# A fixed order for the first 888 operations, product sums in common banks, and the last sums behind the join of two paths

## The chip, the cores and the metric

The kernel runs on one core of one Trainium2 chip. The metric is the device time of one execution in microseconds (us), from the launch to the end of the program. Its engines work side by side, each through its own queue in the order of the program: TensorE (PE) multiplies, VectorE (DVE), ScalarE (ACT) and GpSimd (POOL) work on elements, and SyncE (SP) issues transfers. They wait for each other by semaphores.

## The reference

Attention over 2 batches, 8 heads, 768 positions and 64 numbers per head; a query sees the first 8 keys (global) and the 96 keys that end at its own position (local). Two feed-forward networks follow, on 1536 tokens.

```python
scores = scale * np.matmul(q, k.transpose(0, 1, 3, 2))
keep = is_global | is_local          # pos < 8, or 0 <= rel < 96
dist = np.where(is_global & ~is_local, float(n_local), np.abs(rel))
scores = np.where(keep, scores - slopes[:, None, None] * dist, -1e9)
a = np.exp(scores - np.max(scores, axis=-1, keepdims=True))
a = a / (np.sum(a, axis=-1, keepdims=True) + 1e-09)
x = np.matmul(a, v)                  # then (B, S, H*D): 1536 tokens x 512
h = x @ w_in                         # 512 -> 2048
x = np.where(h > 0, h, np.exp(np.minimum(h, 0)) - 1) @ w_out     # 2048 -> 512
h = x @ w2_in
out = (h * (1 / (1 + np.exp(-1.702 * h)))) @ w2_out
```

`n_global` and `n_local` are inputs too; the kernel reads them on the chip.

## The kernel before

**Products.** Every number of a feed-forward product is split in a high and a low part of a fast 32-bit format, and each product is three matmuls (high by high, high by low, low by high). The weights come as 64-bit floats and are converted on the chip, 128x512 at a time (`conv`): a copy of the upper words into `m` (L414 on ACT or L415 on DVE), three bit operations on DVE (L417, L419, L421), the high part (L247 or L248) and the low part (L254).

**Attention.** There are 12 rows of 128 queries, each in two halves of four heads: 24 units (`Band.unit`). A unit is a chain through the engines: scores (PE, small tiles of 64x64, L345), minus the distance with its minimum (DVE, L670), exponential with its sum (ACT, L674), the sum plus 1e-9 in the small tile `st` (DVE or POOL, L677), its reciprocal (DVE, L680), four scalings of `E` (DVE or POOL, L259), transposes (PE, L693 to L699), copies into `pt` (ACT or DVE, L706), the products with the values (PE, L727 on 128x64 tiles, then L738 on 64x64 tiles), and the split into `xh`, `xl`.

**Feed-forward.** Each network has 4 groups of 512 hidden numbers, each group 3 chunks of 512 tokens. `A` (L447) makes 4 hidden tiles, `B` (L487) sums them onto `acc` or `d` by an add on DVE (L508). The first group's work of chunks 0 and 1 is planned among the attention, so that PE has full tiles (128x128) to multiply while a unit's chain runs elsewhere.

**What sets the order.** `Plan` collects operations as nodes with a due time, one or several engines with a modelled cost, and what they read and write. `run` emits them one by one: the earliest modelled start, among near ones the earliest due; `place` also gives a PSUM bank. The modelled times are in `START`, `WAIT`, `TIMES` and the costs. Where PE would be idle in the model, `idle` emits matmuls on zeros ("fillers", L772) that no one reads. Every engine then works its instructions in this order, however long they really take. Of the 8 banks, 5 are dealt out; bank 5 is kept for the last part of the transposes (`tb`, two halves in turn), banks 6 and 7 for the sums of the products with the values (`xb`).

**The beginning and the end.** `start` sets up distances and slopes and tests `n_global` and `n_local` into `n_flag`; the engines load it (L981) and branch (L986) to `banded`, the path of the profile, or to `general`. At the end of a path each engine jumps to where the paths join; behind it stand only the drains and the last barrier of the program (L1033). The last chunk's four sums are added and stored at the end of the path, the fourth in two halves.

Of the kernel before, what the change touches and what calls it, by code (L numbers as in the profile page):

```python
# [11 lines left out]
F32 = mybir.dt.float32  # L12
# [23 lines left out]
ROW0 = 4.9, 5.8  # L36
# [5 lines left out]
SPARE = 0  # L42
# [18 lines left out]
class Bank:  # L61


    def __init__(self):
        self.left = 0
        self.free_at = 0.0
        self.tile = None


class Node:  # L70
# [3 lines left out]
ENGINES = ("PE", "ACT", "DVE", "POOL", "SP")  # L74
BIAS = dict(DVE=1.373, ACT=0.264, POOL=0.0)
WAIT = {
    "PE": dict(PE=0.0, ACT=0.2, DVE=0.2, POOL=0.22, SP=0.2),
    "ACT": dict(PE=0.27, ACT=0.1, DVE=0.15, POOL=0.17, SP=0.2),
    "DVE": dict(PE=0.25, ACT=0.13, DVE=0.13, POOL=0.16, SP=0.2),
    "POOL": dict(PE=0.2, ACT=0.08, DVE=0.07, POOL=0.02, SP=0.2),  # L80
    "SP": dict.fromkeys(ENGINES, 0.1),
}


class Plan:
# [7 lines left out]
    def __init__(self, k):  # L93
        self.k = k
        self.writer, self.readers = {}, {}
        self.done_at = {}
        self.fill = None
        self.dma = 8.8
        self.avail = dict(START)
        self.banks = [(0.0, i) for i in range(8)]  # L100
        self.pending = {}
        self.cand = {e: [] for e in self.avail}
        self.mode = "full"

    def node(self, due, opts, reads=(), writes=(), alloc=None, uses=(), spare=None, mode="full"):
        n = Node()
        n.mode = mode
# [47 lines left out]
    def at(self, n, e):  # L155
        t = max(n.ready[e], self.avail[e])
        if n.alloc:
# [4 lines left out]
    def run(self):  # L162
        while self.pending:
# [35 lines left out]
    def idle(self, t):  # L199
# [4 lines left out]
        while at + step < t and free[0] + 0.2 <= at:  # L204
# [3 lines left out]
    def place(self, t, e, n):  # L208
# [3 lines left out]
        for b in n.alloc:  # L212
            free = min(self.banks)
# [29 lines left out]
def o_copy(k, out, in_, n, psum=False):  # L243
# [3 lines left out]
        ("ACT", n / 1200 + (0.05 if psum else 0.09), lambda: nc.scalar.activation(out, in_, AF.Copy)),  # L247
# [9 lines left out]
def o_scale(k, out, in_, c, n):  # L257

    op = lambda e: lambda: e.tensor_scalar(out, in_, c, 1.0, ALU.mult, ALU.mult)  # L259
    return [("DVE", n / 1940 + 0.13, op(k.nc.vector)), ("POOL", n / 760 + 0.268, op(k.nc.gpsimd))]  # L260


def start(k, ns, load):
# [9 lines left out]
    lim, off, k.slope = small(2, "n_lim"), small(1, "n_off"), small(H, "slope")  # L273
# [19 lines left out]
    for e in k.E:  # L293
        G.memset(e[:, :, QW:256], 0.0)
# [10 lines left out]
    k.f, k.n, a, c = small(4, "n_f"), small(2, "n_val"), small(2, "n_a"), small(2, "n_c")  # L305
    flag, k.ns = small(1, "n_flag", I32), small(1, "n_scaled")
    V.tensor_copy(k.f, raw)
    V.scalar_tensor_tensor(k.n, k.f[:, 1:4:2], float(2.0 ** 32), k.f[:, 0:4:2], ALU.mult, ALU.add)
    k.ng, k.nl = k.n[:, 0:1], k.n[:, 1:2]
    V.scalar_tensor_tensor(a, k.n, 1.0, lim, ALU.mult, ALU.is_le)  # L310
    for x in range(2):
        V.scalar_tensor_tensor(c[:, x:x + 1], k.n[:, x:x + 1], float(x), a[:, x:x + 1], ALU.is_ge,
                               ALU.mult)
    V.tensor_tensor(flag, c[:, 0:1], c[:, 1:2], ALU.mult)
    V.tensor_scalar(k.ns, k.nl, 1.0 / BIG, 1.0, ALU.mult, ALU.mult)
    V.tensor_scalar(k.big, col, k.ng, 1.0, ALU.is_ge, ALU.mult)
    V.scalar_tensor_tensor(w, own, k.ns, k.big, ALU.is_ge, ALU.mult)
    V.scalar_tensor_tensor(k.d0, own, k.ns, w, ALU.min, ALU.add)
    return flag
# [35 lines left out]
class FFN:  # L355
# [35 lines left out]
    def conv(self, due, G, kind, f):  # L391
# [7 lines left out]
        else:  # L399
# [23 lines left out]
        node(due + 2.5, o_copy(k, hi, mf, 512), [km], khi)  # L423
        node(due + 3, o_sub(k, lo, mf, f32(hi), 512), [km] + khi, klo)

    def A(self, due, G, c, f, t0=0, n=TC):
# [23 lines left out]
        for kk in range(KK):  # L450
            node(due + n / 850 * kk, [("PE", n / 751, lambda kk=kk: mm(kk), 3 * n)],
# [18 lines left out]
    def B(self, due, G, c, m, t0=0, n=TC, late=GF - 1):  # L470
# [5 lines left out]
        b = Bank()  # L476
# [13 lines left out]
        for f in range(GF):  # L490
# [3 lines left out]
            node(at, [("PE", n / 751, lambda f=f: mm(f))],  # L494
# [6 lines left out]
        sc = 1.0 if G < NG else 0.5  # L501
        if g == 0:
# [5 lines left out]
        node(due, [("DVE", n / 960 + 0.07, lambda: V.scalar_tensor_tensor(  # L508
            acc, o(), sc, acc, ALU.mult, ALU.add))], [b] + ka, ka, uses=[b])
# [7 lines left out]
        else:  # L517
            r0 = c * TC + m * 128
            node(due + 0.5, [("SP", 0.33, lambda: nc.sync.dma_start(
                out=self.out[r0:r0 + 128, t0:t0 + n], in_=acc), 0.9)], ka)  # L520
# [28 lines left out]
class Band:  # L549

    def __init__(self, k, plan, pool):
# [5 lines left out]
        self.plan.banks = [(0.0, b) for b in range(5)]  # L557
        self.tb, *self.xb = [Bank() for _ in range(3)]
        for x, b in enumerate((self.tb, *self.xb)):
            b.bank, b.tile = 5 + x, k.bank[5 + x]  # L560
# [11 lines left out]
    def dist(self):  # L572
# [4 lines left out]
        def window():  # L577
            V = nc.vector
            V.scalar_tensor_tensor(base, k.rel, k.ns, k.rel, ALU.is_ge, ALU.add)
            for x in (96, QW + 32):  # L580
                V.tensor_scalar(base[:, x:x + NGLOB], k.big[:, 0:NGLOB], k.ns, 1.0,
                                ALU.max, ALU.mult)

        node(11, [("DVE", 0.65, window)], [("e", 0), ("gt", 1)], [("gt", 0)])
        for n in range(H):
            x = n % 2 * QW
            self.slope(12 + n, k.d[:, n, 0:QW], base[:, x:x + QW], n, QW, [("gt", 0)], [("d", n)])
# [9 lines left out]
    def load(self, r, due):  # L597
        k, node = self.k, self.plan.node
        p = r % 2
        if r < 2:  # L600
            self.plan.given((4.4, 7.0)[r], *self.keys(r))
        else:
            node(due, [("SP", 0.4, lambda: k.load_row(r), 1.6)], writes=self.keys(r))
        if r == 0:
            self.plan.given(8.8, ("v", 0))
            self.plan.given(4.9, "d0")
# [430 lines left out]
```

## Time and profile before

| what | value |
|---|---|
| three runs, median (lowest to highest) | 605.40 us (605.22 to 605.52) |
| profiled execution | 605.43 us |
| its span, first to last instruction | 603.5 us |
| PE busy | 593.2 us (98%), 3675 matmuls |
| DVE busy | 388.9 us (64%) |
| ACT busy | 302.8 us (50%) |
| POOL busy | 68.7 us (11%) |
| DMA | 49.46 MB, mean 82 GB/s |

The profiled execution has 1.9 us outside its span. Busy shares are means over two very different parts: the attention runs until about 109 us, with all four engines at work, and from there only the feed-forward networks are left.

### The profile page before, as it was taken

Reading aid. Unit: us, or ns where it says so; the run is one execution under the profiler, and the core shown is the slowest. Engines: PE = TensorE matmul, PEld = TensorE weight load, DVE = VectorE, ACT = ScalarE, POOL = GpSimd, SP = SyncE. Lnnn points to the kernel's source line nnn. Section 1 sums busy time; section 2 is a strip of 40 time slices with the busy share of each in tenths; the row PEclk is TensorE's granted clock in tenths of the full one; section 3 lists DMA queues with packets and bytes.
Section 4 is the critical chain, followed back from the end, with each engine's and each line's share of the span. In section 5 each row is a group of like instructions: output and inputs, shape, how many; then the busy total and the mean of one; then the engine's idle time right before and its main releaser. Section 6 shows DMA issues by size and latency. Waiting matters only on the chain.

```text
span 603.5 us, 9600 instructions
## 1 busy us (share of the span) xinstructions
PE 593.2 (98%) x3675; PEld 491.0 (81%) x3675; DVE 388.9 (64%) x840; ACT 302.8 (50%) x679; POOL 68.7 (11%) x162
## 2 busy tenths in 40 slices
PE   8999999999999999999999999999999999999996
PEld 6788888888888888888888888888888888888885
DVE  8999896177546983499558953577348843843432
ACT  6998898367245454256447643553324521531220
POOL 7787463000000000000000000000000000000000
PEclk9999999999999999999999999999999999999999
DMA  7666562024201340033002230143003320101012
GB/s 248 227 210 205 159 214 75 1 71 140 71 0 36 109 135 0 1 107 135 38 1 71 98 112 0 36 137 107 1 1 104 106 70 1 35 1 70 18 53 76
DMA packets 20582, 49.46 MB, mean 82 GB/s; under 512 B 1968, under 2 KB 7856, under 8 KB 20528
## 3 DMA queue, kind: packets, MB, share of 16 engines
q1 hardware_dynamic: 20368, 48.51, 24.2%
q8 instruction: 31, 0.51, 0.4%
q10 hardware_dynamic: 160, 0.26, 0.2%
q14 instruction: 23, 0.19, 0.1%
HBM read 45.62 MB, written 3.15 MB: 81 GB/s over the span
## 4 chain that ended last, share of the span: by engine, by line
PE 94%; POOL 3%; DVE 2%; issue 1%; ACT 0%; DVEq 0%; POOLq 0%
PE bank L487 43%; PE bank L447 43%; PE bank L345 2%; PE bank L727 2%; POOL E L259 2%; PE bank L696 1%; PE bank L738 1%; PE bank L699 1%; PE bank L772 0%; DVE E L670 0%; POOL row L621 0%; ACT pt L706 0%; PE bank L693 0%; DVE d L259 0%; POOL st L677 0%
## 5 line engine op out<-in xcount | busy, mean ns | idle before, releaser
L447 PE MATMUL bank<-xh,wbig 128*128 128x512 f32 (+1 forms) x560 | 173.6, 381 | 0.9 <-ACT pt L706 0.5
L447 PEld LDWEIGHTS bank<-xh,wbig 128*128 128x128 f32 x560 | 104.0, 188 | 22.0 <-issue 1.6
L447 PE MATMUL bank<-xl,wbig 128*128 128x512 f32 (+1 forms) x280 | 105.5, 377 | 0.0
L487 PE MATMUL bank<-g,wbig 128*128 128x512 f32 (+1 forms) x360 | 80.8, 367 | 0.2
L447 PE MATMUL bank<-xh,kT 128*128 128x512 f32 x240 | 76.3, 389 | 0.0
L487 PEld LDWEIGHTS bank<-g,wbig 128*128 128x128 f32 x360 | 62.8, 188 | 11.9 <-ACT pt L706 0.3
L508 DVE SCALAR_TENSOR_TENSOR acc<-bank,acc 128x512 f32<-128x512 f32 x48 | 33.2, 692 | 54.0 <-PE bank L487 53.9
L463 ACT ACTIVATE e<-bank 128x512 f32<-128x512 f32 x48 | 28.5, 594 | 68.2 <-PE bank L447 68.1
L447 PEld LDWEIGHTS bank<-xl,wbig 128*128 128x128 f32 x280 | 52.7, 188 | 9.4
L487 PE MATMUL bank<-wbig,g 128*128 128x512 f32 (+1 forms) x246 | 59.8, 384 | 0.0
L254 DVE TENSOR_TENSOR g<-gt,g 128x512 fp32r<-128x512 f32 (+1 forms) x70 | 46.6, 666 | 18.8 <-ACT g L247 17.6
L247 ACT ACTIVATE g<-gt 128x512 fp32r<-128x512 f32 (+1 forms) x70 | 42.6, 609 | 25.0 <-DVE gt L465 15.2
L247 ACT ACTIVATE wbig<-m 128x512 fp32r<-128x512 f32 x39 | 24.6, 630 | 58.2 <-PE bank L447 37.6
L465 DVE SCALAR_TENSOR_TENSOR gt<-e,bank 128x512 f32<-128x512 f32 x48 | 32.9, 685 | 31.1 <-ACT e L463 30.7
L487 PEld LDWEIGHTS bank<-wbig,g 128*128 128x128 f32 x246 | 45.4, 188 | 9.1
L447 PEld LDWEIGHTS bank<-xh,kT 128*128 128x128 f32 x240 | 45.1, 188 | 9.3
L259 POOL TENSOR_SCALAR E<-E,st 128x192 f32<-128x192 f32 (+2 forms) x79 | 47.0, 609 | 9.4 <-DVE st L680 4.7
L460 DVE SCALAR_TENSOR_TENSOR gt<-e,bank 128x512 f32<-128x512 f32 (+1 forms) x52 | 33.4, 643 | 22.1 <-ACT e L458 21.7
L447 PE MATMUL bank<-xl,kT 128*128 128x512 f32 x120 | 46.7, 389 | 0.0
L254 DVE TENSOR_TENSOR wbig<-m,wbig 128x512 fp32r<-128x512 f32 x44 | 30.1, 688 | 23.7 <-ACT wbig L247 22.9
L419 DVE SCALAR_TENSOR_TENSOR raw<-raw 128x512 int32<-128x512 int32 x64 | 44.6, 697 | 0.7
L421 DVE SCALAR_TENSOR_TENSOR m<-m,raw 128x512 int32<-128x512 int32 x64 | 44.3, 692 | 0.9
(129 smaller groups left out, 896.4 us busy)
## 6 DMA issues: line engine op xcount, KB each, us to landing
raw<-in_w1i_dram SPq DMA_DIRECT2D x16, 512.0 KB, 3.5
raw<-in_w1o_dram SPq DMA_DIRECT2D x16, 512.0 KB, 3.4
raw<-in_w2i_dram SPq DMA_DIRECT2D x16, 512.0 KB, 3.3
raw<-in_w2o_dram SPq DMA_DIRECT2D x16, 512.0 KB, 3.3
row<-in_qk_dram SPq DMA_DIRECT2D x9, 512.0 KB, 4.8
v<-in_v_dram SPq DMA_DIRECT2D x12, 256.0 KB, 3.9
va<-in_v_dram SPq DMA_DIRECT2D x10, 256.0 KB, 4.1
out_dram<-acc SPq DMA_DIRECT2D x8, 256.0 KB, 2.0
```

Source lines behind the costliest of these rows:

```text
L247: ("ACT", n / 1200 + (0.05 if psum else 0.09), lambda: nc.scalar.activation(out, in_, AF.Copy)),
L254: return [("DVE", n / 960 + 0.068, lambda: nc.vector.tensor_tensor(out, a, b, ALU.subtract))]
L259: op = lambda e: lambda: e.tensor_scalar(out, in_, c, 1.0, ALU.mult, ALU.mult)
L345: k.nc.tensor.matmul(banks[y // 2 * 2 + x][to, y % 2 * n:y % 2 * n + n], lhsT=v[rows, pr, q + 64 * x:q + 64 * x + 64], rhs=v[rows, pr, c:c ...
L419: node(due + 1, [("DVE", 0.6, lambda: V.scalar_tensor_tensor(top, bot, 29, top, ALU.logical_shift_right, ALU.bitwise_or))], [kr], [kr])
L421: node(due + 1.5, [("DVE", 0.6, lambda: V.scalar_tensor_tensor(m, m, 3, top, ALU.logical_shift_left, ALU.bitwise_or))], [km, kr], [km])
L447: nc.tensor.matmul(h(), lhsT=w[:, kk, :], rhs=x[:, kk, :], start=(kk == 0 and j == 0), stop=(kk == KK - 1 and j == 2))
L460: node(due + 1, [("DVE", n / 960 + 0.07, lambda: V.scalar_tensor_tensor(gt, e, -1.0, h(), ALU.add, ALU.max))], [ke, b], [kg], uses=[b])
L463: node(due, [("ACT", n / 1200 + 0.05, lambda: S.activation(e, h(), AF.Tanh, scale=0.851))], [b], [ke], uses=[b])
L465: node(due + 1, [("DVE", n / 960 + 0.07, lambda: V.scalar_tensor_tensor(gt, e, 1.0, h(), ALU.add, ALU.mult))], [ke, b], [kg], uses=[b])
L487: nc.tensor.matmul(o(), lhsT=lhsT, rhs=rhs, start=(f == 0 and j == 0), stop=(f == GF - 1 and j == 2))
L508: node(due, [("DVE", n / 960 + 0.07, lambda: V.scalar_tensor_tensor(acc, o(), sc, acc, ALU.mult, ALU.add))], [b] + ka, ka, uses=[b])
```

## The change

It has four parts.

1. `ORDER` lists the first 888 operations by number, with a letter for the engine where there is a choice (p, a, v, g, s for PE, ACT, DVE, POOL, SP); `run` places these as listed and plans the rest as before. `START`, `WAIT`, `ROW0`, `TIMES` and several costs have new values, by which the due times of the rest, the fillers and the banks come out. More operations may choose: ACT for the scalings of `E`, POOL for two steps of `conv` in the first group.
2. No bank is kept for `tb` and `xb`. Transposes take two banks and the sums of a row take two from the common eight, and the two keys that kept transposes and products in the order of the units are gone.
3. `start` makes the slopes by one shift of integers on DVE from a POOL iota, in place of 16 POOL memsets, tests the limits on raw integers, and writes two new tables of limits on POOL.
4. The adds and stores of the last chunk's third and fourth sum (`held`) are emitted behind the join of the two paths, for which they have fixed banks.

```diff
-TIMES = (7.0, 3.3, 2.8)
+TIMES = (6.0, 3.3, 3.0)
-START = dict(PE=5.3, ACT=5.0, DVE=5.2, POOL=6.0, SP=5.0)
+START = dict(PE=6.6, ACT=5.05, DVE=5.45, POOL=5.05, SP=5.0)
+ORDER = """
+598 41g 9a 107 0 32a 18g 605 38a 61a 156 12a 35g 10 59 4a 110v 60v 11 13 2g 62 15v 14 19 5g 16
...
+"""
     def run(self):
+        for word in self.order:
+            n = self.nodes[int(word.rstrip(LETTERS))]
+            e = ENGINES[LETTERS.index(word[-1])] if word[-1] in LETTERS else n.opts[0][0]
+            n.spare = 0
+            self.place(self.at(n, e), e, n)
         while self.pending:
...
-    for x, most in enumerate((NGLOB, NWIN + 1)):
-        G.memset(lim[:, x:x + 1], float(most))
-    for n in range(H):
+    for to, values in ((most, (NGLOB, NWIN + 1)), (least, (0, 1))):
+        G.memset(to, 0.0)
         for x in range(2):
-            h = n // 2 * 2 + (n % 2 ^ x)
-            G.memset(k.slope[64 * x:64 * x + 64, n:n + 1], -BIG * 2.0 ** (2 - h))
+            G.memset(to[:, 2 * x:2 * x + 1], float(values[x]))
+    for x in range(2):
+        iota(shift[64 * x:64 * x + 64].rearrange("p (a b) -> p a b", b=2),
+             pattern=[[-2, NP], [2 * x - 1, 2]], base=256 + 127 + 38 + 2 - x, channel_multiplier=0)
...
+    V.tensor_scalar(bits, shift, 23, None, ALU.logical_shift_left)
     V.tensor_scalar(rel, rel, off, 1.0 / BIG, ALU.subtract, ALU.mult)
...
+        slow = [] if G else [
+            ("POOL", 0.66, lambda: nc.gpsimd.tensor_scalar(mf, topf, sc, 1.0, ALU.mult, ALU.mult)),
+            ("POOL", 0.66, lambda: nc.gpsimd.tensor_copy(hi, mf))]
...
+        held = (G, c) == (2 * NG - 1, NCH - 1) and m > 1
+        b = Bank(m + 3 + (t0 > 0) if held else None)
...
+        if held:
+            b.left += 1
+            k.held.append((add, store))
+            return
...
-        self.plan.banks = [(0.0, b) for b in range(5)]
-        self.tb, *self.xb = [Bank() for _ in range(3)]
...
-            node(due + 2.3, o_scale(k, e, e, st[:, 12 + n:13 + n], Ws[x]),
-                 [(kE, n), (kst, 12)], [(kE, n)])
-        ta, tb, ktb = Bank(), self.tb, ("tb", u % 2)
+            c = st[:, 12 + n:13 + n]
+            node(due + 2.3, o_scale(k, e, e, c, Ws[x]) + [("ACT", Ws[x] / 1200 + 0.19, lambda e=e, c=c:
+                 nc.scalar.activation(e, e, AF.Copy, scale=c))], [(kE, n), (kst, 12)], [(kE, n)])
+        ta, tb = Bank(), Bank()
...
-             [ta, ktb, "turn"], alloc=ta, uses=[ta, tb], spare=0)
+             [ta, tb], alloc=[ta, tb], uses=[ta, tb], spare=0)
...
+        plan.order = ORDER.split()
         plan.run()
...
+    for add, store in k.held:
+        add()
+        store()
```

**POOL at the start of the program.** `e` holds the distances by iota, `n_lim` the two limits and `slope` the slopes of the heads; `ident` is the identity for the transposes. Before:

```order
L278 IOTA e_97 128x128
L286 MEMSET n_lim 128x1 x2
L290 MEMSET slope 64x1 x16
masks.py:197 MEMSET ident 128x128
masks.py:199 AFFINE_SELECT ident<-ident 128x128
```

After (`n_shift` is the iota from which DVE shifts the slopes):

```order
L339 IOTA e_97 128x128
L347 MEMSET n_most 128x4
L349 MEMSET n_most 128x1 x2
L347 MEMSET n_least 128x4
L349 MEMSET n_least 128x1 x2
L339 IOTA n_shift 64x8 x2
masks.py:197 MEMSET ident 128x128
```

On DVE the shift that reads `n_shift` (L358) now stands ahead of the first operation on `e`, which before stood first (L295) and needs only the iotas of `e`.

**PE in the later attention, one unit's products between the matmuls of a hidden tile.** `pt` holds the transposed weights of a unit, `v` and `va` the values; L447 and L513 are feed-forward matmuls, L696 and L768 transposes. Before:

```order
L447 MATMUL bank_69<-xh_77,wbig 128x512
L727 MATMUL bank_72<-pt_216,va_106 64x64 x2
L727 MATMUL bank_73<-pt_216,v_104 64x64 x2
L727 MATMUL bank_72<-pt_216,va_106 64x64 x2
L727 MATMUL bank_73<-pt_216,v_104 64x64 x2
L738 MATMUL bank_72<-pt_216,v_104 64x64 x2
L738 MATMUL bank_73<-pt_216,va_106 64x64 x2
L738 MATMUL bank_72<-pt_216,v_104 64x64 x2
L738 MATMUL bank_73<-pt_216,va_106 64x64 x2
L696 MATMUL bank_67<-ident,E_102 128x128 x4
L699 MATMUL bank_71<-ident,E_102 128x128 x2
L447 MATMUL bank_68<-xh_77,wbig 128x512
```

After, the end of a run of four units' products (two rows of queries, with banks of their own):

```order
L811 MATMUL bank_70<-pt_205,v_104 64x64 x2
L811 MATMUL bank_73<-pt_205,va_106 64x64 x2
L799 MATMUL bank_70<-pt_206,va_106 64x64 x2
L799 MATMUL bank_73<-pt_206,v_104 64x64 x2
L799 MATMUL bank_70<-pt_206,va_106 64x64 x2
L799 MATMUL bank_73<-pt_206,v_104 64x64 x2
L811 MATMUL bank_70<-pt_206,v_104 64x64 x2
L811 MATMUL bank_73<-pt_206,va_106 64x64 x2
L811 MATMUL bank_70<-pt_206,v_104 64x64 x2
L811 MATMUL bank_73<-pt_206,va_106 64x64 x2
L513 MATMUL bank_68<-xh_76,kT 128x512
```

Before, each unit's products in this stretch stand between full tiles; after, those of several units stand in one run. Counted in the order of the whole path, PE changes between full and small tiles 85 times before and 69 times after.

**DVE at the end of the program.** The last adds, and the jump to the join (L986, L1063). Before:

```order
L508 SCALAR_TENSOR_TENSOR d<-bank_71,d 128x512
L508 SCALAR_TENSOR_TENSOR d<-bank_72,d 128x512
L508 SCALAR_TENSOR_TENSOR d<-bank_73,d 128x512
L508 SCALAR_TENSOR_TENSOR d<-bank_66,d 128x256
L508 SCALAR_TENSOR_TENSOR d<-bank_68,d 128x256
L986 UNCONDITIONAL_BRANCH
```

After:

```order
L575 SCALAR_TENSOR_TENSOR d<-bank_68,d 128x512
L575 SCALAR_TENSOR_TENSOR d<-bank_71,d 128x512
L1063 UNCONDITIONAL_BRANCH
L575 SCALAR_TENSOR_TENSOR d<-bank_71,d 128x512
L575 SCALAR_TENSOR_TENSOR d<-bank_72,d 128x256
L575 SCALAR_TENSOR_TENSOR d<-bank_73,d 128x256
L1113 UNCONDITIONAL_BRANCH
```

Three adds stand behind the jump, and so do three stores on SP; a second jump follows on both.

## Rows read from the trace of the kernel before

**Rows 1.** Page, part 4: share of the chain of work by engine.

```profile
PE 94%; POOL 3%; DVE 2%; issue 1%; ACT 0%; DVEq 0%; POOLq 0%
```

**Rows 2.** Chain of waits, in order of time: start us, us, what.

```profile
12.36 0.83 PE bank L772 x7
...
119.59 10.88 PE bank L447 x48
...
587.43 10.69 PE bank L487 x57
598.14 0.78 DVE d L508 x2
```

**Rows 3.** Windows: stretch, its length, busy us (count) by engine, PEclk, DMA, GB/s.

```profile
6.00:58.00 52.00, 48.66 (x762) 40.27 (x763) 48.51 (x203) 48.68 (x184) 42.35 (x84) 1.00 0.68 228
58.00:110.00 52.00, 52.00 (x726) 43.23 (x726) 40.64 (x150) 44.24 (x147) 22.11 (x43) 1.00 0.45 145
110.00:590.00 480.00, 480.00 (x2120) 397.54 (x2119) 292.46 (x469) 208.35 (x349) 0.00 (x0) 1.00 0.18 59
20.00:25.00 5.00, 3.88 (x65) 2.72 (x61) 4.97 (x19) 4.63 (x18) 4.46 (x8) 1.00 0.64 217
590.00:603.50 13.50, 8.46 (x49) 7.32 (x47) 3.09 (x6) 0.00 (x0) 0.00 (x0) 0.94 0.25 84
```

**Rows 4.** Lines, PE: the fillers of the whole program.

```profile
L772 PE MATMUL bank<-q1h x33: 279/283/388, 6.9 to 37.6; 128*128 128x256 f32 x33
```

**Rows 5.** Waits, 6 to 58 us: who waited for whom, us in total, times, longest.

```profile
PEld bank L696 <- POOL E L259: 1.8, 4, 0.6
PEld bank L727 <- ACT pt L706: 1.6, 4, 0.8
```

**Rows 6.** Lines, L259 on POOL: scalings of E, ns min/median/max.

```profile
L259 POOL TENSOR_SCALAR E<-E,st x79: 310/541/1372, 10.7 to 103.8; 128x192 f32<-128x192 f32 x67, 128x64 f32<-128x64 f32 x7, 128x128 f32<-128x128 f32 x5
```

**Rows 7.** Timeline of PE, 85 to 92 us: start us, us, instruction.

```profile
86.61 0.39 PE L447 MATMUL bank<-xl,wbig 128*128 128x512 f32 x1
86.84 0.40 PE L447 MATMUL bank<-xh,wbig 128*128 128x512 f32 x1
87.17 0.34 PE L727 MATMUL bank<-pt,va 128*64 128x64 f32 x4
...
87.95 0.23 PE L738 MATMUL bank<-pt,v 64*64 64x64 f32 x2
...
88.00 0.23 PE L738 MATMUL bank<-pt,v 64*64 64x64 f32 x2
88.02 0.22 PE L738 MATMUL bank<-pt,va 64*64 64x64 f32 x2
88.17 0.65 PE L696 MATMUL bank<-ident,E 128*128 128x128 f32 x4
```

**Rows 8.** Timeline of POOL, 0 to 7 us.

```profile
1.03 1.00 POOL L278 IOTA e<- 128x128 f32 x6
1.97 0.31 POOL L286 MEMSET n_lim<- 128x1 f32 x2
2.03 2.57 POOL L290 MEMSET slope<- 64x1 f32 x16
```

**Rows 9.** Timeline of DVE, 0 to 7 us.

```profile
1.75 0.49 DVE L295 TENSOR_SCALAR e<-e,n_off 128x384 f32<-128x384 f32 x1 [0.36 <-POOL e L278]
...
5.47 0.42 DVE L318 SCALAR_TENSOR_TENSOR d<-e,n_scaled,gt 128x192 f32<-128x192 f32 x1
6.27 0.62 DVE L579 SCALAR_TENSOR_TENSOR gt<-e,n_scaled 128x384 f32<-128x384 f32 x1 [0.38 <-DVE d L318]
```

**Rows 10.** Lines of L986, L1033 and L519: branches, last barrier and stores.

```profile
L986 SPq COMPARE_BRANCH  x2: 46/48/49, 5.5 to 599.4; - x2
...
L1033 SPq EVENT_SEMAPHORE  x18: 17/17/28, 5.6 to 603.5; - x18
...
L1033 SPq DRAIN  x3: 7/7/13, 602.7 to 603.0; - x3
...
DMA to landing us min/median/max: 2.0/2.0/3.4
```

More of the change, by code (lines that the diff above doesn't have):

```diff
@@ L77 @@
     "PE": dict(PE=0.0, ACT=0.2, DVE=0.2, POOL=0.22, SP=0.2),
[L78 to L80 removed]
+    "ACT": dict(PE=0.24, ACT=0.13, DVE=0.13, POOL=0.17, SP=0.2),
+    "DVE": dict(PE=0.23, ACT=0.14, DVE=0.12, POOL=0.08, SP=0.2),
+    "POOL": dict(PE=0.25, ACT=0.24, DVE=0.2, POOL=0.1, SP=0.2),
     "SP": dict.fromkeys(ENGINES, 0.1),
 }
+ORDER = """
@@ L156, in at @@
         t = max(n.ready[e], self.avail[e])
+        if n.alloc and n.alloc[0].want is not None:
+            return max([t] + [at + 0.2 for at, i in self.banks if i == n.alloc[0].want]) if any(
+                i == n.alloc[0].want for _, i in self.banks) else 1e9
         if n.alloc:
@@ L203, in idle @@
         free = min(self.banks, default=(1e9, 0))
-        while at + step < t and free[0] + 0.2 <= at:
+        while at + step < t - 0.1 and free[0] + 0.2 <= at:
             self.fill(self.k.bank[free[1]])
@@ L212, in place @@
         for b in n.alloc:
-            free = min(self.banks)
+            free = min(x for x in self.banks if b.want in (None, x[1]))
             self.banks.remove(free)
@@ L272, in start @@
     small = lambda n, nm, dt=F32: cp.tile([128, n], dt, name=nm)
-    lim, off, k.slope = small(2, "n_lim"), small(1, "n_off"), small(H, "slope")
+    off, shift, most, least = small(1, "n_off"), small(H, "n_shift", I32), small(4, "n_most"), small(4, "n_least")
     rel, neg = k.e[0][:, 0:2 * QW], k.gt[0][:, 0:2 * QW]
@@ L501, in B, with store, add @@
         sc = 1.0 if G < NG else 0.5
+        def store():
+            r0 = c * TC + m * 128
+            nc.sync.dma_start(out=self.out[r0:r0 + 128, t0:t0 + n], in_=acc)
+        def add():
+            V.scalar_tensor_tensor(acc, o(), sc, acc, ALU.mult, ALU.add)
+        if held:
+            b.left += 1
+            k.held.append((add, store))
+            return
         if g == 0:
@@ L507, in B @@
             return
[L508 to L509 removed]
+        node(due, [("DVE", n / 960 + 0.07, add)], [b] + ka, ka, uses=[b])
         if g < NG - 1:
@@ L677, in unit @@
         plus = lambda e: lambda: e.tensor_scalar(st[:, 8:12], st[:, 4:8], 1e-9, None, ALU.add)
-        node(due + 2.1, [("DVE", 0.17, plus(V)), ("POOL", 0.27, plus(nc.gpsimd))],
+        node(due + 2.1, [("DVE", 0.17, plus(V)), ("POOL", 0.24, plus(nc.gpsimd))],
             [(kst, 4 + n) for n in range(4)], [(kst, 8)])
@@ L714, in unit @@
             evac(due + 3, pt[:, 0:512], lambda: ta.tile, ta, ta, kp[0], 512)
-        evac(due + 3.2, pt[:, 512:768], lambda: tb.tile[:, tc:tc + 256], tb, ktb, kp[1], 256)
-        cs = 256 * p
-        kx = [("xb", x, p) for x in range(2)]
-        out = lambda x, pr, hd: self.xb[x].tile[64 * hd:64 * hd + 64,
-                                                cs + 64 * pr:cs + 64 * pr + 64]
+        evac(due + 3.2, pt[:, 512:768], lambda: tb.tile[:, 0:256], tb, tb, kp[1], 256)
+        if half == 0:
+            self.xb = [Bank() for _ in range(2)]
+        xb = self.xb
+        out = lambda x, pr, hd: xb[x].tile[64 * hd:64 * hd + 64, 64 * pr:64 * pr + 64]
         def whole_keys():
@@ L743, in unit @@
         kv = [("v", p)] + ([] if first else [("va", p)])
-        node(due + 4, [("PE", 0.25 if first else 0.48, whole_keys)], kv + kp[:1], kx + ["sums"],
-             uses=self.xb, mode="columns")
-        node(due + 4.3, [("PE", 0.25, half_keys)], kv + kp[1:], kx + ["sums"], uses=self.xb, mode="quarters")
+        node(due + 4, [("PE", 0.25 if first else 0.48, whole_keys)], kv + kp[:1], xb,
+             alloc=None if half else xb, uses=xb, spare=XSPARE, mode="columns")
+        node(due + 4.3, [("PE", 0.25, half_keys)], kv + kp[1:], xb, uses=xb, mode="quarters")
         if half == 0:
```

138 lines of the change are left out of this document (92 added, 46 removed).

## The prediction

> **What bounds the kernel now.** I read the chain of waits first. PE makes 94% of it [rows 1], so the time is PE's list of matmuls plus whatever PE loses. From 109 us on the chain is nothing but PE: each step of 48 full-width matmuls takes 10.88 us, so 226.7 ns each, and the pieces follow each other without a hole until the last one, which starts at 587.43 and lasts 10.69 us; two adds of DVE end it at 598.92 [rows 2]. The windows say the same: PE is busy for 480.00 of 480.00 us from 110 to 590, with DVE at 61% and ACT at 43% [rows 3]. Nothing in the change touches the number of these matmuls, so some 480 us of the 605 can't move.
>
> What can move lies in three places, and each has its own limit.
>
> From 6 to 58 us PE is busy for 48.66 of 52.00 us, so 3.3 us idle, while DVE has 48.51 and ACT 48.68: all three are near full, and POOL has 42.35 [rows 3]. PE's busy time there holds 33 fillers [rows 4], seven of which take 0.83 us [rows 2], so 0.119 us each and 3.9 us in all: time in which PE had no real work. Waits that are named: PE waits 1.8 us for POOL's scalings of E and 1.6 us for ACT's copies into `pt` [rows 5]. From 58 to 110 PE is never idle, but 52.00 us busy is not 52.00 us of useful columns: where it goes from full tiles to small ones it loses time. The beginning and the end of the program have single chains, in which no engine is full.
>
> **The change part by part.** The sum is made against the profiled execution, 605.43 us (span 603.5 and 1.93 outside it); that is 0.03 above the median of the runs.
>
> *Mode changes.* Between two full matmuls PE starts 0.23 us apart (86.61, 86.84), from a full one to the first L727 it takes 0.33 (86.84, 87.17): 0.10 more. From the last pair of L738 to the first transpose it takes 0.15 (88.02, 88.17), where inside the burst a pair follows the pair before by 0.05 (87.95, 88.00): 0.10 more [rows 7]. So a burst of small tiles among full ones costs 0.20 us, and a little more where scores stand in it. Counted in the order of instructions, PE changes between full and small tiles 69 times, 85 before: 8 bursts fewer. 8 x 0.20 = 1.6 to 8 x 0.25 = 2.0; I take 1.8. Nearly all of them (6) go behind the 12th unit, where PE is the only bound, so they count in full. Bounds: 2.4 at 0.30 each; 0 if the merged runs make PE wait for a bank at their head. That PE then wants a run's inputs all at once is in the next term.
>
> *The list.* ORDER moves 888 operations, and what they do is done before too. The gain can only be PE's idle time and fillers in 6 to 58. Two engines are relieved, one is loaded: POOL loses 27 of its scalings of `E`, each 0.54 us at the median [rows 6], so 15 us, and 11 of the small sums for `st`, and gets 13 conversions of 512 columns; ACT takes 30 scalings and gives as much away; DVE has 40 instructions more up to the end of the attention, some 11.5 us by the durations in the trace. But up to the 12th unit DVE has 175 instructions where it had 174, and ACT 102 where it had 101. Their idle time, 52.00 - 48.51 = 3.5 and 52.00 - 48.68 = 3.3 us [rows 3], caps what a better order can win in that stretch: 3.4 us. The list holds 23 fillers where there were 33; 10 x 0.119 = 1.2 us that PE needn't pass on zeros. Of the 1.8 us that it waits for POOL [rows 5] three quarters should go with the scalings, 1.3 us. Sum 2.5. Bounds: 3.4 (the cap) and 0 (waits that only move).
>
> *The beginning.* Before, the distances on DVE start at 1.75, after the iotas of `e` [rows 8, 9]. Now the shift for the slopes stands ahead of them on DVE and waits for `n_shift`, which stands behind 6 memsets on POOL. What is queued behind it on DVE is the whole chain to `d0`, and for `d0` wait the first scalings on ACT and POOL, and by them unit 0. Memsets by the 16 of the slopes take 2.57 / 16 = 0.16 us, iotas 1.00 / 6 = 0.17 [rows 8]: 2.03 + 6 x 0.16 + 2 x 0.17 = 3.3 us; if tiny memsets overlap as the two of `n_lim` do with the next line (1.97, 2.03), 2.6. I take 3.0, and 3.1 for DVE's first operation: 1.35 us later than 1.75. The chain to the end of `d0` took 5.89 - 1.75 = 4.1 us [rows 9]; five small operations go and three come, 0.4 us less. So `d0` stands at 6.9, 1.0 later. The 16 memsets that go save nothing, since POOL was done with them at 4.60, before `d0` [rows 8, 9]. PE has no real work with which to cover this besides the scores of row 1, and DVE's and ACT's full lists start later by as much: +1.0. Bounds: +1.7 (3.3, and nothing saved in the chain) and +0.3.
>
> *The end.* SP's branch ends at 599.4, its first drain comes at 602.7 [rows 10], though it only changes blocks: 3.3 us, which cover the last store (issued until 599.4, landing 2.0 us later, so 601.4). After the change SP jumps while PE is still in the last chunk's sums: behind the second sum PE has 12 matmuls of 0.227 us and 24 of half that, 5.5 us, so the second add (0.7 us) ends 4.8 us ahead of PE's end, and behind the jump 3 of the 5 stores remain. So the jump is hidden, and the program ends when the last store has landed: 601.4 and the 0.8 us that the barrier takes (602.7 to 603.5 [rows 10]), 602.2; I allow 0.6 us from the landing to the barrier, which no row shows: 602.8. That is 0.7 less. Bounds: 1.3 less, and 0 if the second jump costs as much as the first did. The Trainium skill (Runtime: NRT & Kernel Launch, section Instruction fetch mechanics) says that a taken branch forces a fetch only if its target lies outside of the two pages that an engine holds. By that rule the second jump, whose target is the very next block, is free, and the sum stays as it is; read as "every jump fetches", the end gives nothing and the sum is 0.7 higher. No row shows a jump to an adjacent block.
>
> 605.43 - 1.8 - 2.5 + 1.0 - 0.7 = 601.4 us.
>
> **The rivals.**
>
> *The list is as good as it can be.* It wins the whole 3.4 us, and the late `d0` is absorbed, because unit 0's first operations have been put in another order too. For it: fillers, the mark of planned idleness, fall by a third. Against it: DVE and ACT would have to be 100% busy for 50 us in a fixed order, and they were 93% so far [rows 3]. 605.4 - 1.8 - 3.4 - 0.7 = 599.5.
>
> *The waits only move.* Engines follow the list whatever really takes long; one late operation (a POOL scaling may take 1.37 us, where the median is 0.54 [rows 6]) holds all behind it. Then the relief of POOL turns into waits for DVE. 605.4 - 1.8 + 1.0 - 0.7 = 603.9.
>
> *DVE becomes the bound of the attention (slower).* From 6 to the last product at 109.1 DVE works 89 us of 103.1 [rows 3], 86%. It gets 11.5 us more, so 100.7. PE's stretch grows too, since more feed-forward matmuls (10.2 us) now stand ahead of the last product: 103.1 + 10.2 - 1.8 - 2.5 = 109.0 us, in which DVE would be busy for 92%. If it can't be over the 86% that it had, the stretch takes 100.7 / 0.864 = 116.5 us, 7.5 more than planned, and the sum is 601.4 + 7.5 = 608.9; at 88% it takes 114.4 and the sum is 606.8. It decides against the change under 89% (113.0 us, where 4.0 us eat the whole gain). For it: units then wait for reciprocals, as they did on other engines, and from 58 on PE has never waited, so that every wait there is new. Against it: up to 58 us DVE did run at 93%, with the same dependences, and later more full tiles are there to fill with. I put it at 607.3 as a middle.
>
> *PE's clock falls early.* The granted clock was 1.00 in 20 to 25 us, where PE was busy for 3.88 of 5.00 us; it was 0.94 only over the last 13.5 us, where PE stands idle for some 5 [rows 3]. With fewer fillers in the first 13 us (21 after, 28 before) and `d0` late, PE may stand for longer there; at half clock from 8 to 16 us its 7 us of work would take up to 4 us more of what it can't hide: 605.4. The Trainium skill (TensorE: Matmul & The Clock Gate, section 1, on the throttle) has an engine that stands idle fall to 1.2 GHz; by that rule the fillers are what holds the clock, and this case gets its chance. The rows of before show PE kept at 1.00 through every early hole, the longest under 0.8 us.
>
> **How the numbers follow.** What differs by 0.2% (1.2 us) can be told from no change, so faster is under 604.2 and slower over 606.6. Forecast, 601.4 with its terms near what I took: 0.40, within 599.8 to 603.2 by itself. The best list, 599.5: 0.18. Waits only move, 603.9: 0.17. DVE as the bound, 607.3: 0.19, of which 0.05 stay under 606.6. Clock, 605.4: 0.04. The rest, 0.02, is a mishap of another sort, counted as slower. Faster: 0.40 + 0.18 + 0.09 (half of 603.9's spread) = 0.67; slower 0.14 + 0.04 (of 603.9's and the clock's upper ends) + 0.02 = 0.20; same 0.13. For 8 in 10 the range leaves out the lower half of the best list and the upper part of DVE's case: 599.0 to 606.6.
>
> **What would show it.** In the profile after, the feed-forward part must still be pieces of 10.88 us. Mode changes: fewer bursts between 60 and 115 us, and PE busy there for 100%. The list: idle PE plus fillers between 7 and 58 fall from 7.2 to under 5 us, and the waits of PE for POOL's scalings to under 0.6. The beginning: DVE's first operation on `e` near 3.1 and `d0` done near 6.9. The end: SP's jump well ahead of PE's last matmul, and 3.3 us between SP's last branch and its drain gone. The forecast is wrong in its sign if PE waits for DVE's minima, reciprocals or `xl` between 60 and 115 us for over 4 us.

## The result and the profile after

The changed kernel takes 599.08 us (median of 6 runs, 598.42 to 600.87), the kernel before 605.91 us beside it. The ratio is 0.9893, with an interval of 0.9880 to 0.9905: faster by 5.8 to 7.3 us, where 4.0 were forecast. Twice more on other occasions the ratio was 0.9875 (0.9857 to 0.9893) and 0.9877 (0.9862 to 0.9892). The profiled execution took 598.42 us with a span of 596.6, so 7.0 us less than that of before.

The chain of waits after the change, its share by engine (page, part 4) and its last two pieces:

```profile
PE 94%; DVE 3%; POOL 1%; ACT 1%; issue 1%; DVEq 0%; POOLq 0%
```

```profile
581.90 10.71 PE bank L554 x57
592.63 0.78 DVE d L575 x2
```

PE still makes 94% of it, but POOL has fallen from 3% to 1% [rows 1]. The last piece of matmuls ends at 592.61, where it ended at 598.12 [rows 2]: 5.5 us were won ahead of that. From the end of the last add to the end of the span it takes 596.6 - 593.41 = 3.2 us, where it took 603.5 - 598.92 = 4.6: another 1.4 us won. These two make the 6.9 us between the spans.

The windows of the changed kernel (stretch, its length, busy us and count by engine, PEclk, DMA, GB/s):

```profile
6.00:58.00 52.00, 50.90 (x791) 43.80 (x790) 51.22 (x216) 48.71 (x189) 38.93 (x70) 1.00 0.73 234
58.00:110.00 52.00, 52.00 (x603) 44.52 (x601) 43.44 (x164) 39.56 (x135) 10.69 (x24) 1.00 0.35 119
110.00:590.00 480.00, 480.00 (x2234) 397.96 (x2234) 300.01 (x484) 206.83 (x348) 0.00 (x0) 1.00 0.19 62
```

Between 6 and 58 us PE is idle for 1.10 us where it was 3.34 [rows 3], and DVE is busy for 51.22 of 52. Not all of the difference is work: in this execution PE runs at 1.2 GHz until 10.9 us (see the last section) and counts as busy for it, so 0.78 us of idle time ahead of 12 us only turned into slower matmuls. From 12 to 58 us idle time falls from 2.57 to 1.10 us. From 58 to 110 PE is busy throughout, as before, with 603 matmuls in place of 726: more of them are full ones and fewer are small. By their columns (0.2267 us for 512 [rows 2]), feed-forward matmuls worth 14.06 us are done by 58 us, 11.22 before; 4 transposes fewer (0.44 us, at 0.11 from start to start) and 16 scores more (0.65 us for 16 in a row) stand beside them. So 2.84 - 0.44 + 0.65 = 3.1 of the 5.5 us were won up to 58 us, and 2.4 behind.

The fillers, and the waits of PE's weight loads (PEld, which can run beside its matmuls) for POOL's scalings and ACT's copies, 6 to 58 us:

```profile
L845 PE MATMUL bank<-q1h x23: 279/283/581, 7.0 to 26.8; 128*128 128x256 f32 x23
```

```profile
PEld bank L768 <- POOL E L320: 1.2, 3, 0.7
PEld bank L799 <- ACT pt L778: 0.7, 3, 0.3
```

```profile
L320 POOL TENSOR_SCALAR E<-E,st x47: 317/430/1376, 10.6 to 105.9; 128x192 f32<-128x192 f32 x40, 128x128 f32<-128x128 f32 x4, 128x64 f32<-128x64 f32 x3
```

The waits fall from 1.8 and 1.6 us [rows 5] to 1.2 and 0.7. POOL scales 47 tiles of E, 79 before, and each is shorter, 430 ns at the median where it was 541 [rows 6]. ACT takes 30 of the 32, at a median of 444 ns.

The beginning, on DVE:

```profile
2.84 0.26 DVE L358 TENSOR_SCALAR n_slope<-n_shift 128x8 int32<-128x8 int32 x1 [1.45 <-POOL n_shift L339]
2.92 0.41 DVE L359 TENSOR_SCALAR e<-e,n_off 128x384 f32<-128x384 f32 x1
...
5.93 0.42 DVE L379 SCALAR_TENSOR_TENSOR d<-e,n_scaled,gt 128x192 f32<-128x192 f32 x1
```

DVE waits 1.45 us for POOL's `n_shift`, starts on `e` at 2.92 instead of 1.75 [rows 9], and `d0` ends at 6.35 instead of 5.89.

The end, on SP (jumps, then the drain that opens the last barrier):

```profile
L1063 SPq COMPARE_BRANCH  x2: 43/46/49, 6.4 to 588.8; - x2
...
L1113 SPq DRAIN  x3: 7/13/130, 595.7 to 596.3; - x3
```

SP jumps at 588.8, 3.8 us ahead of PE's end. Before it jumped at 599.4, behind its last store, and its drain came 3.3 us later [rows 10]. The last store lands 1.4 us after its issue (issued until 593.89, landed at 595.28), where it took 2.1 (599.40, 601.52); from the landing to the end of the span it takes 1.4 us, where it took 2.0, since SP's drain came 1.2 us behind the landing and now comes 0.4 behind it.

### The profile page after: what moved, and what is told of

Its sections match the earlier page's. It is cut to its first block, busy times and chain, and to the rows that moved or that the text cites. A ratio compares the mean times of both kernels' runs of the same rounds, so it can differ in the third digit from the quotient of the medians.

```text
span 596.6 us, 9552 instructions
## 1 busy us (share of the span) xinstructions
PE 590.3 (99%) x3665; PEld 491.8 (82%) x3665; DVE 399.7 (67%) x879; ACT 296.6 (50%) x672; POOL 52.8 (9%) x118
## 4 chain that ended last, share of the span: by engine, by line
PE 94%; DVE 3%; POOL 1%; ACT 1%; issue 1%; DVEq 0%; POOLq 0%
PE bank L554 44%; PE bank L513 44%; PE bank L799 2%; PE bank L408 2%; PE bank L768 1%; PE bank L811 1%; POOL E L320 1%; DVE E L742 1%; PE bank L771 1%; ACT E L746 1%; DVE wbig L315 0%; DVE raw L485 0%; POOL wbig L477 0%; POOL e L339 0%; DVE wbig L309 0%
## 5 line engine op out<-in xcount | busy, mean ns | idle before, releaser
L513 PE MATMUL bank<-xh,wbig 128*128 128x512 f32 (+1 forms) x560 | 171.4, 379 | 0.4 <-DVE st L752 0.4
L513 PEld LDWEIGHTS bank<-xh,wbig 128*128 128x128 f32 x560 | 103.6, 188 | 20.4 <-issue 1.0
L513 PE MATMUL bank<-xl,wbig 128*128 128x512 f32 (+1 forms) x280 | 105.6, 377 | 0.0
L513 PE MATMUL bank<-xh,kT 128*128 128x512 f32 x240 | 77.0, 390 | 0.0
L513 PEld LDWEIGHTS bank<-xl,wbig 128*128 128x128 f32 x280 | 52.7, 188 | 9.4
L513 PEld LDWEIGHTS bank<-xh,kT 128*128 128x128 f32 x240 | 45.1, 188 | 9.4
L308 ACT ACTIVATE g<-gt 128x512 fp32r<-128x512 f32 (+1 forms) x64 | 39.7, 620 | 25.0 <-DVE gt L531 17.2
L308 ACT ACTIVATE wbig<-m 128x512 fp32r<-128x512 f32 x36 | 22.7, 629 | 57.6 <-PE bank L513 35.8
L513 PE MATMUL bank<-xl,kT 128*128 128x512 f32 x120 | 46.7, 389 | 0.0
L746 ACT ACTIVATE E<-E,st 128x192 f32<-128x192 f32 (+2 forms) x96 | 41.4, 436 | 4.4 <-DVE st L742 4.1
L522 ACT ACTIVATE e<-bank 128x512 f32<-128x512 f32 (+1 forms) x52 | 28.9, 560 | 29.6 <-PE bank L513 28.4
```

What stands on the lines that cost most here:

```text
L308: ("ACT", n / 1200 + (0.05 if psum else 0.11), lambda: nc.scalar.activation(out, in_, AF.Copy)),
L513: nc.tensor.matmul(h(), lhsT=w[:, kk, :], rhs=x[:, kk, :], start=(kk == 0 and j == 0), stop=(kk == KK - 1 and j == 2))
L522: node(due, [("ACT", n / 1200 + 0.05, lambda: S.activation(e, h(), AF.Relu, scale=-1.0))], [b], [ke], uses=[b])
L746: node(at + 0.5, [("ACT", W / 1200 + 0.28, lambda n=n, e=e: nc.scalar.activation(e, e, AF.Exp, bias=st[:, n:n + 1], scale=-1.0, accum_out= ...
```

## The experiments

The theory after the result: the time went in three places that add up, the waits and fillers of PE up to 58 us, the changes between full and small tiles behind, and the jump at the end; the late `d0` costs something, but the new order takes more off the same stretch. The rivals: truer costs and common banks do it without the list; the order on PE alone matters, not who scales; and the beginning is hidden. PE's last matmul is compared where a few tenths matter, since what follows it varies from run to run by more (see e2).

**e3: without the list.** All else as in the changed kernel.

```diff
-        plan.order = ORDER.split()
+        plan.order = ()
```

> The changed kernel without the list: its planner chooses the order of all operations, with the new costs, waits and common banks. It has 30 runs of small tiles (18 with the list, 28 before). Theory (the list itself brings the gain up to 58 us, and shorter runs behind): 12 runs at 0.2 us and the waits of the first part back, 4 to 6 us slower than the changed kernel, 603 to 605 us. Rival (truer costs and common banks bring it): within 1.5 us of the changed kernel.

609.81 us, ratio to the kernel before 1.0074 (1.0058 to 1.0090): 11 us slower than the changed kernel and slower than the kernel before. The rival falls. The size that I expected falls too, since it was 4 to 6 us. Its windows:

```profile
6.00:58.00 52.00, 47.01 (x684) 38.44 (x681) 42.93 (x165) 46.11 (x170) 42.37 (x85) 1.00 0.70 224
58.00:120.00 62.00, 61.36 (x799) 49.65 (x801) 41.75 (x163) 50.15 (x170) 22.86 (x53) 1.00 0.38 125
```

DVE is busy for 42.93 us up to 58, where the list keeps it at 51.22, and PE is idle for 5.0. Its last matmul ends 11.3 us after that of the changed kernel. The planner with the new numbers, choices and banks is thus worse than the old one; how much of that the due times make, which were changed along with the list, was not tried.

**e8: the list up to 58 us only.**

```diff
-        plan.order = ORDER.split()
+        plan.order = ORDER.split()[:505]
```

> Only the first 505 entries of the list are used (to about 58 us of the plan); the planner orders what follows, with 24 runs of small tiles in all in place of 18. Theory (what lies behind 58 us is changes between full and small tiles, 0.2 us a run): 1.3 to 2 us slower than the changed kernel, and the same up to 58 us. Rival (behind 58 us the list mostly avoids waits): over 3 us slower, with PE idle between 58 and 120 us.

602.37 us, ratio 0.9957 (0.9943 to 0.9970), 3.5 us slower than the changed kernel by the medians (598.82 in e0); PE's last matmul comes 3.3 us later. Up to 58 us it is the same (feed-forward matmuls worth 14.2 us are done). Behind, there are 6 runs more, and PE is idle a little:

```profile
6.00:58.00 52.00, 50.71 (x793) 43.45 (x791) 50.85 (x217) 49.04 (x190) 37.49 (x71) 1.00 0.71 235
58.00:120.00 62.00, 61.62 (x743) 49.65 (x742) 39.72 (x144) 45.45 (x151) 22.74 (x46) 1.00 0.34 116
```

So neither side has it: 6 runs at 0.22 us (below) are 1.3 us, and the transposes behind 58 us take 8.4 us from start to start in place of 7.1, so 1.3 us more, of which the trace names waits for POOL's scalings (1.1 us of PE's weight loads). The other 0.7 us I can't place. The list's second half is worth both.

**e5: the long runs of small tiles split.** Six feed-forward steps and one step of products are moved in the list; six runs more, no work added.

```diff
-819 820 569 589 524 525 544 572 545 573 592 593
+569 589 524 525 819 544 545 820 572 573 592 593
...
```

(PE's entries of the last run alone; the other moves are 754 behind 380, 766 behind 429, 793 behind 506 and 764 behind 477)

> Only the order on PE changes, behind 58 us: six steps of feed-forward matmuls are moved into the long runs of small tiles, so that there are 24 runs of small tiles in the program where there were 18; no work is added. Theory (each run among full tiles costs 0.2 to 0.3 us of PE): 1.2 to 1.9 us slower than the changed kernel, and no new wait on PE. Rival (what was gained behind 58 us were other things than mode changes): 0 to 0.3 us.

601.74 us, ratio 0.9929 (0.9914 to 0.9943): 2.9 us slower, and PE's last matmul 3.3 us later. More than either expected. The chain shows the two parts, first a new wait and then the price of a split:

```profile
109.28 0.50 ACT pt L778
...
111.34 0.61 PE bank L799 x16
111.95 0.39 PE bank L811 x16
112.34 0.90 PE bank L554 x3
113.24 0.61 PE bank L799 x16
113.86 0.39 PE bank L811 x16
114.25 0.89 PE bank L554 x3
```

Three matmuls of 512 columns take 0.90 us here, where three of 48 take 10.88 x 3 / 48 = 0.68: 0.22 us for going to small tiles and back, twice alike. Six of these are 1.3 us. The rest is the cover that the moved steps had given to ACT's copies: PE stood idle for 1.10 us in front of a transpose, waiting for `pt`, and its weight loads for 1.5. In the changed kernel, the same place, the products of two units stand in one piece of 32:

```profile
110.10 0.61 PE bank L799 x16
110.71 0.39 PE bank L811 x16
111.10 1.08 PE bank L799 x32
112.19 0.62 PE bank L811 x32
112.81 0.62 PE bank L799 x16
113.43 0.39 PE bank L811 x16
```

Two units joined take 1.08 + 0.62 = 1.70 us, where apart they take 2 x (0.61 + 0.39) = 2.00: the change between the two small shapes costs as well, some 0.3 us for a pair. In e5 this pair is apart, which makes 0.3 us of its 3.3 beside 1.3 for the runs and 1.1 to 1.5 for the lost cover; 0.2 to 0.6 us stay open. In the changed kernel eight runs fewer behind 58 us (5, where the kernel before has 13) at 0.22 and one such pair make 2.1 of the 2.4 us won there.

**e10: 16 scalings from ACT back to POOL.** Sixteen that the list gives to ACT up to about 58 us; the order of the list is kept.

```diff
-... 23a ... 97a ... 146a ... 173a ... 195a ...
+... 23g ... 97g ... 146g ... 173g ... 195g ...
```

> The changed kernel with one thing undone: 16 scalings of E that the list gives to ACT before 58 us go back to POOL, at the same places of the list. POOL gets 16 x 0.54 = 8.7 us more in a stretch of 52 in which it is busy for 39. Theory (PE waited for POOL's scalings, and moving them is a good part of the gain up to 58 us): 1.3 to 3 us slower, with waits of PE for scalings back. Rival (the order of the operations brings it, whoever scales): within 0.5 us.

602.79 us, ratio 0.9945 (0.9930 to 0.9960): 4.4 us slower than the changed kernel beside it (598.40), and the last add 5.2 us later. The waits of PE's weight loads for POOL's scalings rise from 1.2 to 5.7 us, and PE itself stands idle for 4.2 of them:

```profile
PEld bank L768 <- POOL E L320: 5.7, 6, 1.3
```

So who scales does matter in this order: without these moves all that the list wins up to 58 us would be gone. What an order made for POOL's scalings would win was not tried. Part of the 5.2 us is the clock. The windows show it (PEclk is the third number from the end):

```profile
50.00:54.00 4.00, 2.13 (x17) 1.66 (x15) 3.20 (x9) 0.79 (x3) 4.00 (x6) 1.00 0.49 182
54.00:58.00 4.00, 3.99 (x60) 3.74 (x62) 2.35 (x12) 2.73 (x12) 2.25 (x4) 0.61 0.02 6
58.00:62.00 4.00, 4.00 (x68) 3.79 (x64) 4.00 (x20) 3.80 (x18) 1.28 (x4) 0.96 0.79 256
```

From 50 to 54 us PE was busy for only 2.13 of 4 us, and then its clock was granted at 0.61 in the mean, so at 1.2 GHz for most of the stretch (from 54.9 to 58.3 us in the trace's record of the clock), and PE was busy all the while. 3.4 us at half speed lose 1.7 us of work; by this estimate the other 3.5 of the 5.2 us are the waits. The four runs agree: two have a mean clock of 0.997 and 0.996 (603.57 and 603.31 us), two of 0.999 (602.03 and 602.27), and these two, which show no such loss, are still 3.6 to 3.9 us slower than the changed kernel.

**e1 and e11: the shift behind the distances.** The line that makes the slopes moves behind the first five instructions on the distances.

```diff
-    V.tensor_scalar(bits, shift, 23, None, ALU.logical_shift_left)
     V.tensor_scalar(rel, rel, off, 1.0 / BIG, ALU.subtract, ALU.mult)
 ...
         V.tensor_copy(own[:, x:x + n], rel[:, at:at + n])
+    V.tensor_scalar(bits, shift, 23, None, ALU.logical_shift_left)
```

> The shift for the slopes stands behind the first operations on the distances, so that DVE need not wait for POOL's iota of shifts: d0 should be done near 5.6 us instead of 6.36. Theory (the late d0 is absorbed by other work up to unit 0's transposes): the time stays within 0.3 us of the changed kernel, and unit 0's transposes stay near 11.6 us. Rival (the beginning is on the path, as the prediction had it): 0.6 to 0.8 us faster, the transposes near 10.9 us.

> e1_shift_later once more, beside the changed kernel on the same chip. Theory (d0 1.1 us earlier is worth 0.7 to 0.9 us at PE's last matmul): a median 0.7 us under that of the changed kernel, if the last stores go alike. Rival (it is absorbed): the same median.

On DVE `d0` now ends 1.1 us earlier than in the changed kernel:

```profile
1.76 0.54 DVE L358 TENSOR_SCALAR e<-e,n_off 128x384 f32<-128x384 f32 x1 [0.38 <-POOL e L339]
...
4.84 0.42 DVE L379 SCALAR_TENSOR_TENSOR d<-e,n_scaled,gt 128x192 f32<-128x192 f32 x1
```

The last add starts at 591.72 and 591.81 in the two profiles; in three of the changed kernel it starts at 592.63, 592.56 and 592.60. So 0.8 us of the 1.1 arrive at PE's end: the beginning is on the path. In time it is 598.10 against 598.82 and 597.98 against 598.40 (ratios to the kernel before 0.9873 and 0.9875, 0.9878 and 0.9877, all with intervals of 0.0015 to 0.0019 to either side), which doesn't tell the two apart. It has the lowest medians and the earliest end of PE of all that was run, and is faster than the kernel before by 1.2 to 1.3%.

**e13: the new beginning alone, in the kernel before.** `start` is taken over as a whole, and nothing else but the three lines of the general path that read what it sets up.

```diff
-    lim, off, k.slope = small(2, "n_lim"), small(1, "n_off"), small(H, "slope")
+    off, shift, most, least = small(1, "n_off"), small(H, "n_shift", I32), small(4, "n_most"), small(4, "n_least")
...
```

> The kernel before with the new beginning alone (slopes by the shift, limits on integers; the shift ahead of the distances). Theory (the beginning lies on the path): d0 0.5 us later than before and the kernel 0.3 to 0.5 us slower than before. The prediction's size: 1.0 us slower. Rival (the beginning is hidden): no difference.

Its last add starts at 598.60, that of before at 598.14: 0.46 us, as late as `d0` was (6.35 against 5.89). In time nothing can be seen, 606.05 against 606.14, ratio 1.0000 (0.9991 to 1.0009). So the theory holds by the profile, one of each kernel, and the 1.0 us of the prediction is excluded.

**e9: 9 matmuls on zeros at the start in place of 6, with the later shift.**

```diff
-NWARM = 6
+NWARM = 9
```

> As e1_shift_later (the shift behind the first operations on the distances), with 9 matmuls on zeros at the start in place of 6. Theory (where the clock of PE rises late, at 10 us instead of near 5, the first units start 0.5 us or more late): the clock is up by 6 us, unit 0's transposes start by 9.9 us, and the time is that of the best runs of e1_shift_later, 597.6, or 0.3 less than its median. Rival (a late clock is hidden by unit 0's chain): the same median as e1_shift_later, 598.1.

599.40 us, ratio 0.9892 (0.9877 to 0.9908): no gain. The clock was up by 5.1 us and unit 0's transposes started at 10.08, but the last add started at 592.12, later than in e1 and e11. e1 and e11 are one kernel: in e1 the clock rose at 5.8 us and the transposes started at 9.81, in e11 at 9.7 and 11.08, and the last add came at 591.72 and 591.81. So a late clock at the start is all but hidden, and the first theory falls; the rival is nearer, though this kernel was even slower than it said, in its profile mostly behind the last add (5.0 us, see e0). Why the last add came 0.3 to 0.4 us later than in those two is not shown.

**e2: the last sums in front of the join again.**

```diff
-        held = (G, c) == (2 * NG - 1, NCH - 1) and m > 1
+        held = False
```

> The last sums and stores stand in front of the join again; all else as in the changed kernel. Theory (the jump was the last thing on the path, all of it): 1.4 us slower than the changed kernel, 4.6 us from DVE's last add to the end of the span in place of 3.2. Rival (the end as the prediction sized it): 0.7 us slower.

599.83 us, ratio 0.9900 (0.9883 to 0.9917), against 598.82 of the changed kernel in the same comparison: 1.0 us, between the two, but the intervals of the two ratios overlap. From the last add to the end of the span it takes 4.4 us, where two of three profiles of the changed kernel have 3.2 and the third, e0, has 4.9 for another reason (below). The last store lands 2.1 us after its issue, not 1.4.

**e4: the held sums alone, in the kernel before.**

```diff
+        if held:
+            b.left += 1
+            k.held.append((add, store))
+            return
...
+    for add, store in k.held:
+        add()
+        store()
```

> The kernel before with one part of the change alone: the last three sums and stores behind the join. Theory (the jump lies on the path, and costs what the profiles differ by): 1.0 us faster than the kernel before, 0 to 1.4 by where fetches of instructions meet the last stores. Rival (as the prediction sized it): 0.7 us. Rival (the gain at the end needs the new order): no difference.

605.40 us (12 runs), ratio 0.9993 (0.9981 to 1.0006): 0.4 us faster by the ratio, with an interval from 1.2 faster to 0.4 slower. Inconclusive for the size, though its profile has 3.5 us behind the last add where the kernel before has 4.6.

**e0 and e12: the changed kernel again.**

> The changed kernel once more, so that the others have it on their own chip. Both theories: 598 to 601 us, some 6.5 us under the kernel before.

> The changed kernel on the same chip, for comparison: 598 to 601 us, PE's last matmul near 592.6 us; the rest depends on whether the last store waits behind a fetch of instructions.

598.82 us (597.65 to 600.10) and 598.40 us (597.96 to 598.88). The profile of e0 is one of the long runs, and the difference lies behind the last add:

```profile
592.56 0.78 DVE d L575 x2
```

```profile
L1113 SPq DRAIN  x3: 7/13/131, 597.3 to 597.9; - x3
```

The adds end as in the first profile, the drain comes 1.6 us later (597.3, not 595.7). In the trace's transfers the last nine packets of the last store start at 595.71, right when a fetch of instructions ends, which ran from 594.50 to 595.71; in the first profile a like fetch started at 594.85, and all packets of stores were through at 594.94. Of the 11 profiles with held sums two have this (e0, and e9 with a fetch from 594.26 to 595.29), with 4.9 and 5.0 us behind the last add; nine have 3.2 to 3.5. The three without held sums have 4.4 to 4.6.

## Why the prediction was right

The direction and the places were right. All four terms erred to the same side, too small in their gain or too large in their loss, by 0.5 to 1.1 us each, so that 6.8 us were won where 4.0 were forecast. The range held by luck: 599.08 lies 0.08 us above its lower end, and the medians of e0 and e12 (598.82, 598.40) lie below it.

- *Mode changes*, forecast 1.8 us: 2.4 us behind 58 us. The price per run was right (0.20 to 0.25; measured 0.22 twice). The count was right by luck: 85 and 69 are the changes between all three shapes of tile (128x128, 128x64 and 64x64). Between full and small tiles alone PE changes 56 times before and 36 after, so 28 runs became 18, ten fewer and not eight; but two of the ten lie ahead of 58 us, and eight behind it, where PE is the only bound. What I left out is the change between the two small shapes, 0.3 us where two units' products are joined.
- *The list*, forecast 2.5 us, with 3.4 as the cap: 3.1 up to 58 us with the loss of the beginning already off, so nearer to 3.4 to 3.6 by itself (0.46 us in e13; 0.3 by e1, where 1.1 us of `d0` were worth 0.8). Idle PE and fillers together fell from 7.2 to 4.9 us (1.10 + 1.86 + 16 x 0.119), just under the 5 that I had named. DVE did go to 98.5% (51.22 of 52), which I had held against the best case. The relief of POOL was a right cause: 16 scalings put back cost 5.2 us at the last add (e10). What I had mis-sized is the term of the waits, 1.3 us for POOL's scalings alone: these went from 1.8 to 1.2 us, so by 0.6 and not to under 0.6, but the waits for ACT's copies, which I had left out, went by 0.9 (1.6 to 0.7). POOL also lost 32 scalings (79 to 47), not 27. The order as a whole keeps DVE fuller, and without it all is lost (e3).
- *The beginning*, forecast 1.0 us lost: `n_shift` came 0.2 us earlier than I took (2.81), the chain to `d0` got 0.7 us shorter (2.92 to 6.35) instead of 0.4, and `d0` was 0.46 late. In the kernel before that costs 0.46 us (e13). The term that was mis-sized is the sum of these two steps: six small memsets and both iotas took 0.8 us (2.05 to 2.81) where I took 1.0, and DVE's small operations that went were worth more than I gave them. That the shift's place costs was right: it is 0.8 us in the changed kernel (e1, e11).
- *The end*, forecast 0.7 us: 1.4 by the profile, 1.0 by the times of e2, and 0.4, not clear of none, in e4. The first bound (1.3) was near the truth where no fetch stands in the way. The allowance held: from the landing to the end I took 0.6 + 0.8 us, and it is 1.37. The term that was mis-sized is the landing, 2.0 us after the last store's issue by rows 10; it is 1.4 us in all nine profiles with held sums and no fetch in front, and 2.1 in the three without held sums. There a fetch of 0.45 to 0.61 us starts within some 0.1 us of SP's jump, while the store's packets go out, and they go out over 1.5 to 1.6 us instead of 1.0: the jump seems to have cost twice, by its own 2.9 to 3.2 us and by holding up the store. No run separates the two. The jump to the adjacent block showed no stall: DVE's drain ends at 593.47, 0.06 us behind its last add. The rule of the Trainium skill (Runtime: NRT & Kernel Launch, section Instruction fetch mechanics), that only a target outside of the held pages is fetched, agrees with that; the reading "every jump fetches" does not.
- *The rivals.* DVE as the bound did not come: behind 58 us PE was never idle, with DVE at 84% (43.44 of 52). The clock's case came in part, and nearly free of charge: in eight of the eleven profiles with the new list or its planner PE ran at 1.2 GHz until 9.6 to 10.9 us, which cost 0.1 us at the last add (e11 beside e1). Fewer fillers can't be why the early rise failed, since up to 5.9 us, when it was up in all the others, PE's instructions are the same. All three profiles of the old order rose early, the one with the new beginning too (e13); what makes the difference stays open. The best list, 599.5, came nearest to the time; I gave it 0.18.

## What to carry to other kernels

Where one engine is the bound and its neighbours are near full, look at who does the small shared work: sixteen small scalings put back on a neighbour in its way cost 4.4 us here. Count how often the matrix engine changes between full and small tiles (and these apart from changes among small ones), and put small work into few long runs, but leave beside each run what covered its inputs: a split cost 0.22 us here, and a lost cover 1.1 us. A wait that a small helper operation brings to the front of a queue (here the shift of eight slopes) delays the whole chain behind it; place it where its input is long ready.

## What the hardware showed that I had not expected

**The clock at the start varies from run to run.** With the same six matmuls on zeros and the same scores behind them, full speed came at 4.3 to 5.9 us in five profiles and at 9.6 to 10.9 us in eight, by the trace's record of the clock. The column PEclk doesn't show this for the first stretch, but the matmuls do: seven fillers took 1.86 us in the changed kernel and 1.09 us in e1.

```profile
7.01 1.86 PE L845 MATMUL bank<-q1h 128*128 128x256 f32 x7
```

```profile
6.91 1.09 PE L845 MATMUL bank<-q1h 128*128 128x256 f32 x7
```

The Trainium skill (TensorE: Matmul & The Clock Gate, Part 1) says that the moment of the rise depends on the run; the runs agree. It gives half a microsecond to either side; here e1 and e11, one and the same kernel, are 3.9 us apart (5.8 and 9.7).

**Fetches of instructions can hold up data.** In two of the eleven profiles with held sums the last nine packets of the last store start only when a fetch of 1.0 to 1.2 us ends, and 4.9 and 5.0 us stand behind the last add, where the other nine have 3.2 to 3.5. That the two share a DMA engine is argued from these times; the trace's transfers don't name one. Of the changed kernel's 14 runs three were profiled, one of them with this wait (600.10 us, against 598.42 and 598.40); its 1.6 us are half of the spread of all 14 (597.65 to 600.87 us), but that the other long runs have it too is not shown.
